# Partial sums and outputs of a matmul chain go through GpSimd's DMA queue

## The chip, the cores and the metric

One core of a Trainium2 chip runs the whole program. The metric is the device time of one execution in microseconds. Engines are named as the profile names them: PE (TensorE), DVE (VectorE), ACT (ScalarE), POOL (GpSimd) and SP (SyncE, which only issues DMAs).

## The reference

Attention through packed keys, then two feed-forward blocks, all in float32; 4608 tokens (8 batches of 576), model width 512.

```python
p_packed = softmax(p @ k.T / 8) @ v          # per head: 32 packed rows
a = softmax(q @ p_packed.T / 8) @ p_packed   # per head; 4608 x 512 in all
x = ((a @ w1) * (a @ w2)) @ w3 @ w_out       # 512 -> 1024 -> 1024 -> 512
h = x @ w_in                                 # 512 -> 2048
out = max(0.01 * h, h) @ w_out2              # 2048 -> 512
```

## The kernel before, in words

The program has two halves. The first (up to about 690 us) does the attention and the first feed-forward block and leaves `x2d`, the input of the second block, transposed, in DRAM. The change does not touch it. The last stage (lines 762 to 985) does the second block.

**Products.** A product of two float32 numbers is made of three fp32r matmuls (high x high, high x low, low x high; `PASSES`). Each matrix product is cut into 2 x 2 blocks and done with seven block products instead of eight (a Strassen-Winograd scheme), so operands come as seven "forms" m = 1 to 7, each a high and a low tile: `xh`, `xl` for the input, `wi` and `wo` for the weights, `gh`, `gl` for the activations. `ORDER` is the order of the seven products.

**Units.** The work is 18 units t = 0 to 17. The hidden width is cut into three parts F = 0, 1, 2 (`PARTS`; three, three and two chunks), and each part goes over the six token tiles of 768 columns (`NB = 6`). `h_unit(t)` makes the hidden activations of a unit (first matmuls, then leaky ReLU on ACT), `g_ops(t)` makes their seven forms on DVE and ACT, and `o_unit(t)` multiplies by `wo` and adds into four tiles `o` of 128 x 768 (384 KB each). Since the sum over hidden width is cut in three, the `o` of part 0 is stored to `part[0]` in DRAM, that of part 1 is fetched from `part[0]`, added to and stored to `part[1]`, and that of part 2 is fetched from `part[1]`, added to and stored to `out`. `begin_o(t)` allocates the four tiles and issues the fetches (line 936), the end of `o_unit(t)` issues the four stores (line 955). The pool holds `OB = 4` tiles `o`, one unit's worth: a fetch for the next unit needs a tile whose store has landed.

**Order.** The loop at line 959 does `begin_o(t-1)`, `h_unit(t)`, half of the loads of the next input forms, `o_unit(t-1)`, the other half, and `g_ops(t)`; the last unit of a part has its own `o_unit` directly behind that of the unit before. The Python order is a priority only: a list scheduler in the build sets the order on each engine from its own time estimates, so moving a DMA to another engine also changes the order of other instructions. On an engine, and on a queue, instructions are issued in that order; one that waits holds up what stands behind it.

**Queues.** In the last stage SP issues everything: the form loads (`load_forms`, line 797, `XF = 4` tiles each for `xh` and `xl`, seven forms a unit, so most loads wait for PE to be done with an older form), the weights (lines 787 and 825), the staging of later input tiles (lines 670 and 674, up to about 900 us), and the fetches and stores of `o`. POOL has nothing to do after 580.4 us. A matmul chain of `sevens` writes PSUM tiles `a`, `b` and `c` (2, 3 and 3 buffers); the additions into `o` and `gr` are DVE's (lines 842 and 847), some first copies are ACT's (line 844). DVE does in the last stage nothing but two-operand additions and subtractions.

Of the kernel before, what the change touches and what calls it, by code (L numbers as in the profile page):

```python
# [32 lines left out]
def tile_kernel(ctx, tc, qT, kT, vL, pT, w12, w3b, wo1, win, wo2, out):  # L33
    nc = tc.nc
# [599 lines left out]
    UT = 2 * HT  # L634
# [183 lines left out]
    part = dram.tile([2, DM, NT], F32, name="part")  # L818
# [60 lines left out]
    def run(dst, pairs, first, last):  # L879
        total = 3 * len(pairs)  # L880
        n = 0
        for lhs, rhs in pairs:
            for l, r in PASSES:
                nc.tensor.matmul(  # L884
                    dst, lhs(l), rhs(r), start=first and n == 0, stop=last and n == total - 1, skip_group_check=True
                )
                n += 1
# [39 lines left out]
    def begin_o(t):  # L927

        F, c0 = t // NB, t % NB * UT
        outs[t] = []  # L930
        for mb in range(2):
            for i in range(2):
                r = slice(i * 256 + mb * P, i * 256 + mb * P + P)
                o = b2.tile([P, 2, HT], F32, tag="o", name="o", bufs=OB)
                if F:
                    nc.sync.dma_start(out=o, in_=part[F - 1, r, c0:c0 + UT].rearrange("p (j c) -> p j c", j=2))
                outs[t].append((o, (out if F == 2 else part[F])[r, c0:c0 + UT].rearrange("p (j c) -> p j c", j=2)))

    def o_unit(t):
        F, n = t // NB, PARTS[t // NB][1]  # L940
        G = ops.pop(t)
        todo = outs.pop(t)
        chains = []
        for mb in range(2):
            def product(m, dst, first, last, mb=mb):
                run(
                    dst,
                    [(lambda l, c=c: wo[m][:, l, c, mb * P:mb * P + P], lambda l, c=c: G[m][l][:, c]) for c in range(n)],
                    first, last,
                )  # L950

            chains.append((product, lambda i, j, mb=mb: todo[2 * mb + i][0][:, j], F > 0))
        sevens(chains, None)
        for x in (1, 3, 0, 2):
            nc.sync.dma_start(out=todo[x][1], in_=todo[x][0])

    load_forms(0, ORDER[4:])
    STAGED = {0: ((3, 0),), 1: ((3, 1), (4, 0)), 2: ((4, 1), (5, 0)), 3: ((5, 1),)}
    for t in range(TB):
        F = t // NB  # L960
        start, end = t % NB == 0, t % NB == NB - 1
        if not start:
            begin_o(t - 1)
        if t == 0:
            load_wo(F)
        h_unit(t)
        if start:
            if t:
                load_wo(F)
            make_wo(F)  # L970
        if t + 1 < TB:
            load_forms(t + 1, ORDER[:4])
        if not start:
            o_unit(t - 1)
        if t + 1 < TB:
            load_forms(t + 1, ORDER[4:])
        g_ops(t)
        for f in (stage_b(*ua) for ua in STAGED.get(t, ())):
            for step in f:
                step()  # L980
        if end:
            begin_o(t)
            o_unit(t)
            if t + 1 < TB:
                make_wi(F + 1)
# [43 lines left out]
```

## Time and profile before

| | |
|---|---|
| device time, 3 runs | 1377.09, 1381.65, 1386.25 us; median 1381.65 |
| the profiled execution | 1377.09 us, of which 1375.3 us from the first instruction to the last |
| PE matmul busy | 1314.8 us (96%) |
| DVE, ACT, POOL busy | 956.6 us (70%), 703.3 us (51%), 185.8 us (14%) |
| DMA, all queues | 323.48 MB, mean 235 GB/s |
| SP's queue (q1) | 300.74 MB; its packets took 65.6% of the 16 DMA engines' span |

How to read it: the profiled execution took 1377.09 us, 4.56 us less than the median of the three runs. The granted clock of PE was 0.99 of 2.4 GHz over the span. A share of busy time is a mean over stages with different limits; the sections below go to the last stage alone. In a timeline row, the number in square brackets at the end is the time for which the engine stood idle before the first instruction of the row, and what ended that. SP's rows have no such number: the time between two of its rows is waiting. A row of busy time by stretch has: the stretch and its length in us; busy us (and number of instructions) of PE, PEld (weight loads), DVE, ACT and POOL; PE's granted clock; the DMA engines' busy share; GB/s. A row of waits has: who, for whom, us in total, times, the longest.

### The profile page before, as it was taken

To read this page: it belongs to the slowest core of one execution; us is meant where nothing else is said; L and a number is where in the kernel's file an instruction comes from. 1 tells how busy PE (TensorE), PEld (TensorE's weight loads), DVE (VectorE), ACT (ScalarE), POOL (GpSimd) and SP (SyncE) were. 2 spreads that over 40 slices of the span, in tenths; PEclk is the share of its full clock that TensorE was granted. 3 is DMA by queue.
4 is the path that set the end of the run, shared out by engine and by line. 5 is a ranking of instruction groups with operands and counts; after the bars stand their busy time and mean duration, and the time that the engine had idled before them with its cause. 6 is when DMAs were issued, how large, how long until landed. Compare 5 with 4: busy or idle time off the path is not lost.

```text
span 1375.3 us, 23473 instructions
## 1 busy us (share of the span) xinstructions
PE 1314.8 (96%) x8512; PEld 1256.7 (91%) x8512; DVE 956.6 (70%) x1588; ACT 703.3 (51%) x1365; POOL 185.8 (14%) x148
## 2 busy tenths in 40 slices
PE   6789999989999999999999999999999999999998
PEld 3578889988898999999999999998999999999997
DVE  4989777586778767863786676658665468496667
ACT  3576444565567545753755555536433335254432
POOL 1544540352025302300000000000000000000000
PEclk9899999999999999999999999999999999999999
DMA  9798785487777774187878975558447655778884
GB/s 291 261 314 290 238 278 181 119 273 253 250 229 248 243 236 153 47 273 251 278 256 297 322 280 206 203 177 283 152 160 240 207 175 181 256 276 306 290 288 149
DMA packets 174835, 323.48 MB, mean 235 GB/s; under 512 B 22656, under 2 KB 93312, under 8 KB 174720
## 3 DMA queue, kind: packets, MB, share of 16 engines
q1 hardware_dynamic: 153984, 300.74, 65.6%
q10 hardware_dynamic: 20736, 21.24, 4.5%
q8 instruction: 67, 1.10, 0.3%
q14 instruction: 48, 0.39, 0.1%
HBM read 226.75 MB, written 95.16 MB: 234 GB/s over the span
## 4 chain that ended last, share of the span: by engine, by line
PE 74%; DMA 10%; DVE 7%; issue 2%; ACT 1%; SPq 0%; POOL 0%; ACTq 0%; DVEq 0%; POOLq 0%
PE mm L105 26%; PE b L884 24%; PE c L884 13%; PE a L884 6%; DMA xh<-xfd 3%; PE m L105 2%; PE at L163 2%; DVE cT L282 1%; DMA xl<-xfd 1%; DVE M L108 1%; DVE cT L279 1%; DMA c<-wo 1%; PE at L215 1%; DMA c<-w3b 1%; DMA wi<-wid 1%
## 5 line engine op out<-in xcount | busy, mean ns | idle before, releaser
L105 PE MATMUL mm<-AT,M 128*128 128x288 f32 x1536 | 234.0, 304 | 22.5 <-DVE ab L451 11.1
L105 PEld LDWEIGHTS mm<-AT,M 128*128 128x128 f32 x1536 | 213.4, 192 | 36.3 <-DVE ab L451 14.3
L884 PE MATMUL b<-xh,wi 128*128 128x384 f32 x768 | 218.1, 336 | 6.2 <-DMA xh<-xfd 4.1
L884 PE MATMUL b<-gh,wo 128*128 128x384 f32 x768 | 213.6, 335 | 1.4 <-DVE o L847 1.4
L105 PEld LDWEIGHTS mm<-ab,W 128*128 128x128 f32 x1536 | 205.1, 189 | 7.7 <-issue 5.2
L105 PE MATMUL mm<-ab,W 128*128 128x288 f32 x1536 | 210.7, 297 | 1.3 <-DVE ab L108 1.3
L884 PEld LDWEIGHTS b<-xh,wi 128*128 128x128 f32 x768 | 140.5, 188 | 8.7 <-DMA xh<-xfd 4.5
L884 PEld LDWEIGHTS b<-gh,wo 128*128 128x128 f32 x768 | 140.3, 188 | 2.0 <-issue 1.0
L884 PE MATMUL b<-xl,wi 128*128 128x384 f32 x384 | 128.6, 335 | 0.0
L884 PE MATMUL b<-gl,wo 128*128 128x384 f32 x384 | 128.4, 334 | 0.0
L108 POOL TENSOR_TENSOR wsp<-c,wsp 128x512 fp32r<-128x512 f32 x54 | 73.2, 1358 | 279.1 <-ACT wsp L380 253.3
L656 ACT CAST gh<-gr 128x1152 fp32r<-128x1152 f32 (+1 forms) x72 | 75.6, 1052 | 68.9 <-PE b L884 32.2
L884 PE MATMUL c<-xh,wi 128*128 128x384 f32 x384 | 106.4, 336 | 3.3 <-DMA xh<-xfd 3.1
L884 PE MATMUL c<-gh,wo 128*128 128x384 f32 x384 | 107.3, 335 | 0.1
L108 DVE TENSOR_TENSOR gl<-gr,gh 128x1152 fp32r<-128x1152 f32 (+1 forms) x72 | 87.5, 1221 | 22.6 <-ACT gh L656 22.6
L108 DVE TENSOR_TENSOR M<-m,M 64x512 fp32r<-64x512 f32 x124 | 84.7, 686 | 22.8 <-ACT M L414 20.0
L656 ACT CAST gh<-gs 128x1152 fp32r<-128x1152 f32 (+1 forms) x54 | 56.9, 1054 | 61.7 <-PE b L884 32.3
L285 POOL TENSOR_TENSOR c<-cT,c 128x512 int32<-128x512 int32 x56 | 76.7, 1376 | 62.7 <-DVE cT L282 25.3
L832 ACT ACTIVATE gr<-gr 128x1152 f32<-128x1152 f32 (+1 forms) x54 | 57.3, 1062 | 47.9 <-DVE gr L847 47.6
L414 ACT CAST M<-m 64x512 fp32r<-64x512 f32 x124 | 71.5, 580 | 18.6 <-DVE M L108 5.4
L108 DVE TENSOR_TENSOR ab<-ab,ab 128x288 fp32r<-128x288 f32 x128 | 66.7, 550 | 15.2 <-ACT ab L430 14.9
L844 ACT COPY gr<-b 128x384 f32<-128x384 f32 x96 | 45.7, 479 | 58.2 <-PE b L884 56.8
(142 smaller groups left out, 2389.4 us busy)
## 6 DMA issues: line engine op xcount, KB each, us to landing
xh<-xfd SPq DMA_DIRECT2D x126, 384.0 KB, 5.3
xl<-xfd SPq DMA_DIRECT2D x126, 384.0 KB, 5.0
part<-o SPq DMA_DIRECT2D x48, 384.0 KB, 2.8
o<-part SPq DMA_DIRECT2D x48, 384.0 KB, 4.2
c<-wo SPq DMA_DIRECT2D x24, 512.0 KB, 5.7
c<-w12d SPq DMA_DIRECT2D x48, 256.0 KB, 3.5
abd<-ab ACTq DMA_DIRECT2D x80, 144.0 KB, 4.5
ab<-abd SPq DMA_DIRECT2D x80, 144.0 KB, 3.5
```

The costliest lines, as they stand in the source:

```text
L105: nc.tensor.matmul(dst, lhs(i), rhs(j), start=first and n == 0, stop=last and n == 2)
L108: engine.tensor_tensor(out=out, in0=x, in1=rd(hi), op=ALU.subtract)
L163: nc.tensor.matmul(ps[r:r + 64, th, :TH], w[:, 2 * g + j, :], x[:, th * TH:th * TH + TH], start=True, stop=True)
L215: nc.tensor.matmul(ps[r, :P], PT[:K, c, r], v[j][:K, c, :], start=c == 0, stop=c == 4)
L279: nc.vector.tensor_scalar(out=t, in0=hw, scalar1=3, scalar2=0x3FFFFFFF, op0=ALU.logical_shift_left, op1=ALU.bitwise_and)
L282: nc.vector.scalar_tensor_tensor(out=t, in0=hw, scalar=0xC0000000, in1=t, op0=ALU.bitwise_and, op1=ALU.bitwise_or)
L285: return lambda: nc.gpsimd.tensor_tensor(out=q, in0=t.bitcast(I32), in1=q, op=ALU.add)
L414: nc.scalar.copy(m[r, 0], ps[h ^ n][r])
L656: nc.scalar.copy(hi[step], x[step])
L832: nc.scalar.activation(out=out, in_=x, func=AF.Prelu, alpha=0.01)
L844: nc.scalar.copy(out, ps)
L884: nc.tensor.matmul(dst, lhs(l), rhs(r), start=first and n == 0, stop=last and n == total - 1, skip_group_check=True)
```

## The change

Two words change: the fetches of old partial sums and the stores of `o` are issued by POOL (`nc.gpsimd`) and no longer by SP (`nc.sync`). Sizes, buffers and semaphores' meaning stay.

```diff
--- before.py
+++ after.py
@@ begin_o
                 o = b2.tile([P, 2, HT], F32, tag="o", name="o", bufs=OB)
                 if F:
-                    nc.sync.dma_start(out=o, in_=part[F - 1, r, c0:c0 + UT].rearrange("p (j c) -> p j c", j=2))
+                    nc.gpsimd.dma_start(out=o, in_=part[F - 1, r, c0:c0 + UT].rearrange("p (j c) -> p j c", j=2))
@@ o_unit
         sevens(chains, None)
         for x in (1, 3, 0, 2):
-            nc.sync.dma_start(out=todo[x][1], in_=todo[x][0])
+            nc.gpsimd.dma_start(out=todo[x][1], in_=todo[x][0])
```

There are 48 fetches and 72 stores (48 of `part`, 24 of `out`). Numbers in the names below are those of the buffers; four `o` numbers in a row are the four tiles of one unit.

SP in the middle of part 1, while the tiles `o_12212` to `o_12218` of unit 8 are stored and those of unit 9 (`o_12596` to `o_12602`) are fetched; before:

```order
L936 DMA o_12596<-part_8477 128x768
L936 DMA o_12598<-part_8477 128x768
L797 DMA xl_12550<-xfd_78 128x768
L955 DMA part_8477<-o_12214 128x768
L797 DMA xh_12549<-xfd_78 128x768
L936 DMA o_12600<-part_8477 128x768
L955 DMA part_8477<-o_12218 128x768
L797 DMA xl_12554<-xfd_78 128x768
L797 DMA xh_12553<-xfd_78 128x768
L936 DMA o_12602<-part_8477 128x768
L797 DMA xh_12557<-xfd_78 128x768
L797 DMA xl_12558<-xfd_78 128x768
```

The same form loads on SP in the change:

```order
L797 DMA xl_12550<-xfd_78 128x768
L797 DMA xh_12549<-xfd_78 128x768
L797 DMA xl_12554<-xfd_78 128x768
L797 DMA xh_12553<-xfd_78 128x768
L797 DMA xl_12558<-xfd_78 128x768
L797 DMA xh_12557<-xfd_78 128x768
L797 DMA xl_12768<-xfd_78 128x768
L797 DMA xh_12767<-xfd_78 128x768
L797 DMA xl_12772<-xfd_78 128x768
L797 DMA xh_12771<-xfd_78 128x768
```

The stores and fetches have left, and the form loads stand one behind the other in nearly the old order (the last low and high form are swapped).

The end of the program: before, on SP, the stores of the last unit but one (`o_14956` to `o_14962`), the fetches and stores of the last (`o_15218` to `o_15224`):

```order
L955 DMA out<-o_14956 128x768
L936 DMA o_15218<-part_8477 128x768
L955 DMA out<-o_14960 128x768
L936 DMA o_15220<-part_8477 128x768
L955 DMA out<-o_14958 128x768
L955 DMA out<-o_14962 128x768
L936 DMA o_15222<-part_8477 128x768
L936 DMA o_15224<-part_8477 128x768
L955 DMA out<-o_15218 128x768
L955 DMA out<-o_15220 128x768
L955 DMA out<-o_15222 128x768
L955 DMA out<-o_15224 128x768
```

In the change, on POOL:

```order
L955 DMA out<-o_14956 128x768
L955 DMA out<-o_14960 128x768
L955 DMA out<-o_14958 128x768
L936 DMA o_15218<-part_8477 128x768
L936 DMA o_15220<-part_8477 128x768
L936 DMA o_15222<-part_8477 128x768
L955 DMA out<-o_14962 128x768
L936 DMA o_15224<-part_8477 128x768
L955 DMA out<-o_15218 128x768
L955 DMA out<-o_15220 128x768
L955 DMA out<-o_15222 128x768
L955 DMA out<-o_15224 128x768
```

The first two fetches of the last unit stood each behind one store; now three stores stand ahead of the first three fetches. The last fetch still stands behind all four stores.

PE at the end of the program, where `c_15280` is the product that ends with the addition into the last fetched tile, `o_15224`; before:

```order
L884 MATMUL b_15234<-gh_15197,wo6_8472 128x384
L884 MATMUL c_15280<-gh_15210,wo3_8476 128x384
L884 MATMUL c_15280<-gl_15211,wo3_8476 128x384
L884 MATMUL c_15280<-gh_15210,wo3_8476 128x384 x2
L884 MATMUL c_15280<-gl_15211,wo3_8476 128x384
L884 MATMUL c_15280<-gh_15210,wo3_8476 128x384
L884 MATMUL b_15234<-gh_15206,wo7_8474 128x384
L884 MATMUL b_15234<-gl_15207,wo7_8474 128x384
L884 MATMUL b_15234<-gh_15206,wo7_8474 128x384 x2
L884 MATMUL b_15234<-gl_15207,wo7_8474 128x384
L884 MATMUL b_15234<-gh_15206,wo7_8474 128x384
L884 MATMUL b_15234<-gh_15214,wo4_8475 128x384
```

In the change:

```order
L884 MATMUL b_15226<-gh_15214,wo4_8475 128x384
L884 MATMUL b_15226<-gl_15215,wo4_8475 128x384
L884 MATMUL b_15226<-gh_15214,wo4_8475 128x384 x2
L884 MATMUL b_15226<-gl_15215,wo4_8475 128x384
L884 MATMUL b_15226<-gh_15214,wo4_8475 128x384
L884 MATMUL c_15280<-gh_15210,wo3_8476 128x384
L884 MATMUL c_15280<-gl_15211,wo3_8476 128x384
L884 MATMUL c_15280<-gh_15210,wo3_8476 128x384 x2
L884 MATMUL c_15280<-gl_15211,wo3_8476 128x384
L884 MATMUL c_15280<-gh_15210,wo3_8476 128x384
L884 MATMUL b_15234<-gh_15214,wo4_8475 128x384
```

The last part of the product `c_15280` (with `wo3`) stood twelve matmuls ahead of the end; now it stands six ahead of it.

## Rows read from the trace of the kernel before

**Rows 1.** Busy time by stretch: parts 0, 1, 2 of the last stage, and the end.

```profile
690.00:968.00 278.00, 273.62 (x1565) 271.12 (x1565) 186.36 (x270) 152.22 (x256) 0.00 (x0) 1.00 0.72 250
968.00:1196.00 228.00, 226.00 (x1292) 223.88 (x1290) 142.55 (x201) 88.05 (x123) 0.00 (x0) 1.00 0.57 191
1196.00:1359.00 163.00, 159.18 (x905) 157.23 (x906) 117.23 (x191) 70.38 (x111) 0.00 (x0) 1.00 0.78 273
1359.00:1376.00 17.00, 10.73 (x56) 9.28 (x55) 8.50 (x15) 0.84 (x1) 0.00 (x0) 0.93 0.54 199
```

**Rows 2.** Waits of PE, 690 to 1376 us.

```profile
PE b L884 <- DMA xh<-xfd: 4.1, 4, 1.5
PE c L884 <- DMA xh<-xfd: 3.1, 3, 1.4
...
PE b L884 <- DVE o L847: 1.4, 2, 0.7
PE b L884 <- DVE o L842: 0.6, 1, 0.6
...
PE c L884 <- DMA xl<-xfd: 0.4, 2, 0.2
```

**Rows 3.** Waits of SP, the same stretch.

```profile
SPq L955 <- DVE o L847: 137.0, 29, 17.8
SPq L797 <- PE b L884: 86.2, 50, 6.7
SPq L936 <- DMA part<-o: 38.1, 19, 5.4
SPq L936 <- DMA out<-o: 35.4, 15, 6.9
```

**Rows 4.** SP's timeline, 1077 to 1091 us: start, length, instruction.

```profile
1077.99 0.38 SPq L955 DMA_DIRECT2D part<-o  x1
...
1083.63 0.32 SPq L936 DMA_DIRECT2D o<-part  x1
...
1088.37 0.32 SPq L936 DMA_DIRECT2D o<-part  x1
1088.78 0.38 SPq L797 DMA_DIRECT2D xh<-xfd  x1
```

**Rows 5.** PE's timeline: four matmuls that waited for a form.

```profile
936.76 0.44 PE L884 MATMUL c<-xh,wi 128*128 128x384 f32 x1 [1.41 <-DMA xh<-xfd]
...
1093.74 0.80 PE L884 MATMUL c<-xh,wi 128*128 128x384 f32 x3 [0.73 <-DMA xh<-xfd]
...
1197.37 0.45 PE L884 MATMUL b<-xh,wi 128*128 128x384 f32 x1 [1.51 <-DMA xh<-xfd]
...
1339.26 0.44 PE L884 MATMUL c<-xh,wi 128*128 128x384 f32 x1 [1.00 <-DMA xh<-xfd]
```

**Rows 6.** Busy time by stretch, the turn from part 1 to 2.

```profile
1190.00:1206.00 16.00, 13.66 (x74) 12.32 (x72) 6.59 (x13) 7.70 (x15) 0.00 (x0) 1.00 1.00 368
```

**Rows 7.** Lines 936 (fetch) and 955 (store): ns min/median/max of an issue; us to landing.

```profile
L936 SPq DMA_DIRECT2D o<-part x48: 319/320/555, 916.9 to 1362.5; - x48
...
DMA to landing us min/median/max: 3.2/4.2/7.7
...
DMA to landing us min/median/max: 2.3/3.1/7.7
```

**Rows 8.** Lines 285 (POOL) and 279 (DVE): ns min/median/max.

```profile
L285 POOL TENSOR_TENSOR c<-cT,c x56: 1260/1292/1932, 31.2 to 537.8; 128x512 int32<-128x512 int32 x56
...
L279 DVE TENSOR_SCALAR cT<-c x72: 387/427/1518, 9.0 to 460.4; 128x512 uint32<-128x512 uint32 x72
```

**Rows 9.** Waits of DVE, 690 to 1376 us: those for a fetch.

```profile
DVE o L842 <- DMA o<-part: 10.7, 7, 2.2
```

**Rows 10.** The end: timeline of SP (last stores) and of DVE (last addition).

```profile
1364.40 8.05 SPq L955 DMA_DIRECT2D out<-o  x4
...
1371.53 0.56 DVE L842 TENSOR_TENSOR o<-b,o 128x384 f32<-128x384 f32 x1 [1.42 <-PE b L884]
```

## The prediction, made before the changed kernel was run

> **What bounds the kernel now.** I read the busy time by stretch first, since the change acts in the last stage alone. In its three parts PE works 273.62 of 278 us, 226.00 of 228 and 159.18 of 163 [rows 1]; the reader is to see that 10.2 us are all that PE leaves idle there, at the full clock. Only the last 17 us have more (6.3 us), most of it behind the last matmul. So this stage is PE's own work, and no rearrangement of DMAs can give back more than those 10.2 us and a little of the end.
>
> The waits of PE come next. Form loads (`xh`, `xl`) cost it 4.1 + 3.1 + 0.4 = 7.6 us in nine waits; additions into `o` that came late cost 1.4 + 0.6 = 2.0 us [rows 2]. These two are what the change can touch.
>
> Then SP's waits: 137.0 us for an addition that must end before a store, 38.1 + 35.4 us for a store that must land before a fetch reuses its tile, and 86.2 us for PE to give a form tile back [rows 3]. The last would stay; the first three, 210 us, hold form loads behind them only where a form tile is free meanwhile. SP's timeline shows one such place: a store goes out at 1077.99, the fetch that needs its landing stands until 1083.63, the next such fetch until 1088.37, and only then, at 1088.78, goes the load of a high form [rows 4]. PE waits for it until 1093.74, for 0.73 us [rows 5].
>
> **What moves and what it costs.**
>
> *The form loads.* 120 DMAs leave SP. Their issue, 0.32 us each [rows 7], was 38 us of SP's time and is worth nothing by itself: SP has hundreds of us of waiting. What counts is the standing. Of PE's waits for forms, three (1.41 us at 936.76, 0.73 at 1093.74, 1.00 at 1339.26 [rows 5]) follow the pattern of [rows 4], a fetch that waits for a landing a few loads ahead on SP, of which there are these three; I take all of their 3.1 us back. The other 4.5 us I take back by half, 2.2 us: there SP did not stand for a landing just before, and the load was slow to land, with stores and fetches ahead of it in the same queue. The clearest, 1.51 us at 1197.37 [rows 5], lies in a stretch where the DMA engines are busy all of the time, at 368 GB/s [rows 6]: the bytes stay, so not all of it can go. Gain: 5.3 us, with bounds of 0 and 7.6.
>
> *What a transfer costs on POOL.* No row shows a DMA that POOL issues. I call p the time by which one lands later than from SP. Below: landings reach 7.7 us against a least of 3.2 for a fetch and 2.3 for a store [rows 7], because form loads stand ahead in the queue; on a queue of its own a transfer could land sooner, and with medians of 4.2 and 3.1 that is p = -0.8 to -1.0 us. Above: POOL's nearest work, one instruction on 128 partitions, takes 1.29 us, up to 1.93 where DVE is at the same time at work [rows 8]; if making the transfer takes that in place of 0.32 us, p is 1.0 to 1.6 us, and 2.9 if it also stands behind one just like it. I take p = 1.0 us, by the row's median, since mostly one transfer is made at a time. The Trainium skill ("DMA: Bandwidth & Descriptors", section Latency and other measured facts) gives about 1 us to the first byte from GpSimd against 0.6 from SP; with that p would be 0.4 us and the sum 2.5 us lower; no row here shows it.
>
> *The turn of a tile `o`.* Store, landing, fetch, landing, first addition: each turn has two transfers, so 2p = 2.0 us more. In parts 0 and 1 most turns have time: what a fetch brings is used much later, and only seven additions in the whole stage waited for one, for 10.7 us in all [rows 9], at five units (t = 11, 13, 14, 16 and 17), while PE lost 2.0 us by `o` [rows 2]: a fifth. PE has three buffers each of `b` and `c` to run ahead into. Four of these units (the last is counted below) at 2.0 us make 8.0 us more waiting of DVE, and by that fifth 1.6 us of PE. Bounds: 0, if the landings get as much quicker as p costs, and 8.0, if PE's slack is used up.
>
> *The end.* Last addition at 1371.53, last store behind it [rows 10]: that store lands p later, 1.0 us, with nothing to hide it. Ahead of it, the last fetched tile has a turn of 2p = 2.0 us more, while the order gives its product six matmuls more time, at 159.18 / 905 = 0.18 us each [rows 1] 1.1 us: 0.9 us remain. That the first fetch of the last unit now stands behind the store of `o_14958` costs, I think, nothing: the additions into it stand later on DVE too; its cover is the order, and if that is wrong it is one landing of 3.2 to 4.2 us [rows 7]. Sum of the end: 1.9 us.
>
> *Sum.* -5.3 + 1.6 + 1.9 = -1.8 us, on the profiled execution's 1377.09 us 1375.3. That execution was 4.56 us under the median of its three runs; I apply the change to the median, 1381.65 - 1.8 = 1379.9, and say **1380 us**.
>
> **The rivals.**
>
> *A. As above, no change that can be measured:* 1380 us. With the gain at 7.6 us, the turns at nothing and the last store 0.8 us sooner it is 1373; with no gain, the turns at 8.0 us and the end at 1.9 it is 1392. Chance 0.56. About 1%, 13.8 us, is what a measurement of this kernel tells from no change.
>
> *B. The forms come no sooner.* SP's loads wait 86.2 us for PE's tiles [rows 3], which no queue changes, and the bytes stay. Then the gain is 0 and the costs 3.5 us: 1385 us. Against it speak [rows 4], where the load stood behind two landings. Beside it stands a rule of the Trainium skill ("DMA: Bandwidth & Descriptors", section Issuing engines are not separate DMA queues): all queues run on the same 16 engines, and issuing from more of them saves only the issuing time. By that rule B is the whole story; the trace agrees for 1190 to 1206 us and speaks against it at 1077 to 1089, where a queue stood still for a semaphore. Chance 0.20.
>
> *C. Slower: the turn of `o` becomes the bound.* The place is part 2 and the turn from part 1 to 2, where additions already wait for fetches [rows 9]. POOL makes its transfers while DVE works, and where both worked at once in this trace each held up the other: POOL's instruction takes 1.29 us in the middle and up to 1.93, DVE's 0.43 and up to 1.52 [rows 8]. On top of that POOL's queue holds a fetch behind stores that are not ready. With p = 2.9 us and PE losing all that DVE loses, five turns of 2p make 29 us and the last store 2.9; less the 5.3 of the forms that is +26.6 us: 1408 us. It decides against no change from 11p = 13.8 + 5.3, p = 1.7 us. For it: the seven waits, and that PE's slack of some us at each is unknown. Against: PE lost only a fifth of what DVE lost, and the landings get a queue of their own. The Trainium skill ("SBUF — State Buffer", section Who interferes with whom) says that GpSimd is shut out only by DVE's two-port modes or, where it reads, by two SBUF inputs, and infers that descriptors escape a `tensor_tensor`, which is all that DVE does in this stage; by that rule p stays near 1 us and C does not happen; no run here shows it yet. Chance 0.16.
>
> *D. Faster, all waits gone:* both lines of waits, 7.6 + 2.0 us [rows 2], go and the end costs nothing: 1372 us. Against: that asks for p below 0 in a stage with 0.78 of the DMA engines busy [rows 1]. Chance 0.07; a time more than 13.8 us lower would ask for more than PE's idle 10.2 us and is as good as excluded.
>
> *E. It does not do what it says:* the order shows the stores and fetches on POOL and no longer on SP, so only an order elsewhere that happens to be worse or better could be the cause. Chance 0.01.
>
> **How the numbers follow.** Predicted is A's time, 1380 us. The range 1370 to 1396 holds A with its bounds, B, D and the lower part of C, and leaves out C's upper part and noise at the low side, less than 2 in 10. Slower by over 1% (above 1395.5) is C but for its lower part, 0.13, and a bit of B: 0.14. Faster by over 1% (below 1367.8) is only a chance of the order: 0.03. Within 1%: 0.83.
>
> **What would show it.** In the changed profile, PE's waits for `xh` and `xl` fall from 7.6 to some 2 to 3 us, and SP waits almost only for PE; if they stay at 7, B is right. The fetch line, now on POOL, shows landings: a median under 5.2 us (4.2 + p) agrees with p up to 1 us; 6 us and more is C, and DVE's waits for fetches then go from 10.7 us to over 30. PE's busy time in the last stage stays where it is within 1 us, and DVE's additions keep their 0.56 us. The last store lands about 1 us later behind the last addition. What would make the prediction wrong is a PE that waits for `o` in every unit of part 2, or a first fetch of the last unit that comes so late that the end stands for it.

## The result, and the profile after

The changed kernel took 1386.94 us (median of 9 runs, 1382.83 to 1390.94), the kernel before 1379.24 us beside it: a ratio of 1.0068, 95% interval 1.0048 to 1.0088. By the ratio it is 9 us slower (the medians are 7.7 us apart), within 1%, where 1.8 us less were forecast. A second measurement (e15 below) gave 1.0045, 1.0027 to 1.0063. The profiled execution took 1387.15 us and spans 1385.4 us, 10.1 more than before. Of these, 0.9 us lie ahead of the stage that the change touches: its first matmul starts at 653.1 us, before at 652.2. In e15, the same program, it starts at 647.9, so moments and lengths of two executions are to be held against each other with care.

Busy time by stretch, with the columns of [rows 1]; the last stretch ends with the program:

```profile
690.00:968.00 278.00, 272.77 (x1558) 269.98 (x1557) 186.02 (x269) 152.09 (x255) 15.35 (x28) 1.00 0.72 249
968.00:1196.00 228.00, 224.02 (x1278) 221.37 (x1278) 143.15 (x202) 84.56 (x117) 24.12 (x44) 1.00 0.55 187
1196.00:1359.00 163.00, 159.25 (x905) 156.86 (x905) 113.69 (x186) 71.16 (x113) 20.26 (x37) 1.00 0.78 275
1359.00:1386.00 27.00, 17.43 (x88) 16.17 (x86) 13.86 (x24) 3.35 (x4) 6.01 (x11) 0.86 0.53 173
```

PE lost 0.9 us more in part 0 and 2.0 us more in part 1; the end is 10 us longer. Part of that length is work which the delays ahead pushed into it: 88 matmuls fall into it, not 56. Its mean granted clock is 0.86 instead of 0.93; over half of what is missing lies behind the last matmul, where it costs nothing (0.65 from 1380 to 1386 us).

PE's waits, to be held against [rows 2]:

```profile
PE b L884 <- DMA xh<-xfd: 6.7, 6, 2.9
PE b L884 <- DVE o L842: 3.2, 2, 2.3
PE c L884 <- DMA xh<-xfd: 2.3, 3, 1.4
...
PE b L884 <- DMA xl<-xfd: 0.7, 1, 0.7
```

With two small rows that are left out (0.2 us for a form, 0.5 us for `o`) the forms cost 9.9 us (7.6 before) and late additions into `o` 3.7 us (2.0 before). SP's waits, beside [rows 3]:

```profile
SPq L797 <- PE b L884: 126.4, 54, 5.4
SPq L797 <- PE a L884: 117.8, 17, 23.3
SPq L797 <- PE c L884: 58.1, 31, 6.1
```

SP is freed as the change meant: the 210 us of waits for additions and landings are gone. What grew is its waiting for PE to give tiles back; the row for `b` stood at 86.2 us. And the line that fetches and the line that stores, now on POOL, beside [rows 7]:

```profile
L936 POOL DMA_DIRECT2D o<-part x48: 548/553/557, 920.6 to 1372.5; - x48
...
DMA to landing us min/median/max: 3.5/5.8/7.9
...
L955 POOL DMA_DIRECT2D part<-o x48: 542/544/689, 715.0 to 1201.2; - x48
...
DMA to landing us min/median/max: 2.6/3.6/9.0
```

A transfer holds POOL for 0.55 us (SP: 0.32), and in the best case lands 0.3 us later than from SP (3.5 against 3.2, 2.6 against 2.3). A store also starts 0.3 us after its addition: the last addition ends at 1379.85 + 0.56 = 1380.41, the store starts at 1380.71; before, both stood at 1372.1.

```profile
1379.85 0.56 DVE L842 TENSOR_TENSOR o<-b,o 128x384 f32<-128x384 f32 x1 [0.49 <-PE b L884]
```

Undisturbed, p is therefore 0.6 us. The medians rose by more, 4.2 to 5.8 and 3.1 to 3.6 us.

### The profile page after: what moved, and what is told of

Its sections match the earlier page's. It is cut to its first block, busy times and chain, and to the rows that moved or that the text cites. A ratio compares the mean times of both kernels' runs of the same rounds, so it can differ in the third digit from the quotient of the medians.

```text
span 1385.4 us, 23473 instructions
## 1 busy us (share of the span) xinstructions
PE 1319.2 (95%) x8512; PEld 1260.5 (91%) x8512; DVE 959.1 (69%) x1588; ACT 702.8 (51%) x1365; POOL 249.9 (18%) x268
## 4 chain that ended last, share of the span: by engine, by line
PE 65%; DMA 12%; DVE 8%; issue 5%; ACT 2%; POOL 1%; SPq 1%; ACTq 0%; POOLq 0%; DVEq 0%
PE mm L105 22%; PE b L884 22%; PE c L884 11%; PE a L884 6%; DMA xh<-xfd 5%; DMA c<-win 2%; PE m L105 2%; PE at L163 1%; PE at L215 1%; DVE M L108 1%; DMA xl<-xfd 1%; DVE cT L282 1%; DVE cT L279 1%; DMA c<-w3b 1%; DVE gl L108 1%
## 5 line engine op out<-in xcount | busy, mean ns | idle before, releaser
L955 POOL DMA_DIRECT2D part<-o x48 | 26.3, 547 | 517.7 <-DVE o L847 484.8
```

The costliest lines, as they stand in the source:

```text
L955: nc.gpsimd.dma_start(out=todo[x][1], in_=todo[x][0])
```

## The experiments

All ratios are to the kernel before, from runs on the same chip. "The turn" in the table is that from unit 6 to 7, the first at which both stores and fetches run; its numbers are the landing of the high form that PE wants next there, and PE's idle time in front of it, both from the trace. An interval is about 2.5 us to either side, and the waits of two executions of one program differ by some us, so a profile alone does not decide a total; a wait that comes back at the same place in every kernel of a kind is taken as its doing.

| run | on POOL | ratio (95%) | landing, us | PE idle, us |
|---|---|---|---|---|
| before | nothing | 1 | 6.3 | 0 |
| the change | all | 1.0068 (1.0048 to 1.0088) | 9.8 | 2.9 |
| e15 | all, again | 1.0045 (1.0027 to 1.0063) | 8.8 | 1.8 |
| e1 | all but the last unit's fetches | 1.0037 (1.0022 to 1.0052) | 10.3 | 3.4 |
| e5 | all but the end | 1.0017 (0.9997 to 1.0038) | 9.2 | 2.2 |
| e4 | units of parts 0 and 1 | 1.0028 (1.0012 to 1.0045) | 9.1 | 2.2 |
| e16 | that turn alone | 1.0027 (1.0010 to 1.0045) | 9.3 | 0.9 |
| e12 | all but end and part 1's fetches | 1.0002 (0.9982 to 1.0021) | 6.4 | 0 |
| e7 | stores of parts 0 and 1 | 0.9988 (0.9970 to 1.0006) | 6.2 | 0 |
| e2 | all stores | 1.0028 (1.0008 to 1.0048) | 5.8 | 0 |
| e3 | all fetches | 1.0059 (1.0036 to 1.0081) | 8.3 | 0 |
| e13 | the end alone | 1.0026 (1.0007 to 1.0045) | 6.3 | 0 |
| e14 | the end alone, on ACT | 1.0000 (0.9982 to 1.0019) | 6.3 | 0 |
| e8 | all, on ACT | 1.0009 (0.9989 to 1.0029) | 7.0 | 0 |

In e2, e7 and e12 the order on SP puts this high form ahead of its low form; the low form then lands 7.3, 7.8 and 7.7 us after its own issue. From the first issue of the pair to the later landing it is 6.7 us before, 7.7 to 8.1 us in these three and 10.3 us in the change, so their rows look better than they are.

Four names run through the expectations: **order** (three stores now stand ahead of the last unit's first fetches), **making** (a transfer that POOL makes comes late), **sharing** (a second queue shares the DMA engines with the form loads) and **packets** (POOL's packets are the larger ones, so its queue gets the larger share).

### The end

**e1, last fetches back on SP.**

```diff
-                    nc.gpsimd.dma_start(out=o, in_=part[...
+                    (nc.sync if t == 17 else nc.gpsimd).dma_start(out=o, in_=part[...
```

> Only the four fetches of the last unit (t = 17) go back to SP; all stores and the other fetches stay on POOL. The changed kernel was 1.0068 times the kernel before (about +9 us). In its trace PE waits 3.7 us for additions into o in the last 20 us, then runs nine matmuls at 0.32 us in place of 0.17, and 5.6 us follow its last matmul in place of 3.8. Theory 'order' (three stores stand ahead of the first three fetches of the last unit on POOL): with nothing ahead of them the fetches land in time, PE's waits for o at the end fall below 1.5 us, the slow matmuls go, the time is 3 to 4 us under the change (ratio to before near 1.004); the last store is still 0.5 us or more late. Theory 'making' (POOL's transfers are late by themselves): the fetches now come from SP but wait for landings of stores made by POOL, so half of it comes back, 1 to 2 us (1.0055). Theory 'sharing' (a second queue takes DMA time from the form loads): nothing at the end hangs on it, 1.0068 stays.

Measured: 1.0037, as order expected. PE's waits for `o` fell to 1.4 us, but the run moved the end in another way too: POOL issues the last three stores together (1377.24 to 1378.85), and the program ends 6.3 us behind the last addition (before: 3.2). **e5, the last stores too**, in the order of the changed kernel:

```diff
+                    (nc.sync if t == 17 else nc.gpsimd).dma_start(out=o, ...
+            (nc.sync if t >= 16 else nc.gpsimd).dma_start(out=todo[x][1], ...
```

> The stores of units 16 and 17 and the fetches of unit 17 are on SP; all else is on POOL as in the change. On SP the build puts the same three stores ahead of the first three fetches as on POOL in the change. 'Order': PE still waits 2 to 4 us for o in the last 20 us, and only the tail behind the last matmul shortens, by about 1 us: ratio near 1.006. 'Making': transfers by SP land 0.3 us and more sooner each and the issue takes 0.3 us less, so PE's waits for o at the end go back to 1.5 us and the tail to 4 us: ratio near 1.003. 'Sharing': the rest of the stage is unchanged, so PE's waits for xh and xl stay at 9 to 11 us whatever the end does.

Measured: 1.0017, below what order expected and near making; PE's waits for forms were 5.8 us, not the 9 to 11 that sharing expected. SP issued the last transfers in the same order as POOL had, three stores ahead of three fetches, and most of the cost was gone: order falls as its cause. The first eight of the same twelve transfers, first on POOL in the changed kernel (timeline: start, length, instruction, idle time before it and what ended that):

```profile
1357.78 0.55 POOL L955 DMA_DIRECT2D out<-o  x1 [11.03 <-DVE o L847]
1359.98 1.08 POOL L955 DMA_DIRECT2D out<-o  x2 [1.65 <-DVE o L847]
1361.29 0.55 POOL L936 DMA_DIRECT2D o<-part  x1 [0.23 <-DMA out<-o]
1363.74 0.55 POOL L936 DMA_DIRECT2D o<-part  x1 [1.89 <-DMA out<-o]
1367.24 0.56 POOL L936 DMA_DIRECT2D o<-part  x1 [2.95 <-issue]
...
1372.45 0.55 POOL L936 DMA_DIRECT2D o<-part  x1 [4.11 <-DMA out<-o]
```

and then on SP in e5:

```profile
1355.80 3.42 SPq L955 DMA_DIRECT2D out<-o  x3
1359.71 2.65 SPq L936 DMA_DIRECT2D o<-part  x3
1363.71 0.34 SPq L955 DMA_DIRECT2D out<-o  x1
1366.88 0.32 SPq L936 DMA_DIRECT2D o<-part  x1
```

From the first store to the last fetch SP takes 11.1 us, POOL 14.7 us. One piece of that is the third fetch: its store had landed at 1364.4 by the trace, yet POOL stood until 1367.24, for 2.95 us that ended with nothing that the profile shows. What hangs on it, on PE in the changed kernel:

```profile
1371.83 0.69 PE L884 MATMUL b<-gh,wo 128*128 128x384 f32 x1 [2.27 <-DVE o L842]
1372.32 0.52 PE L884 MATMUL b<-gl,wo 128*128 128x384 f32 x1
```

After the 2.27 us of idleness the matmuls come 0.32 us apart instead of 0.17 until 1374.9, and the granted clock is 0.66 in the mean:

```profile
1371.00:1376.00 5.00, 4.17 (x15) 4.17 (x16) 2.83 (x6) 0.00 (x0) 1.09 (x2) 0.66 0.53 172
```

With two levels, 2.4 and 1.2 GHz, that mean makes 3.4 us at the lower one; eight steps took 2.6 us in place of 1.4, 1.2 us on top of the wait. e15 has the same behind its wait, 3.4 us at the lower level from 1363.5.

**e13, the end alone on POOL**, and **e14, the end alone on ACT's queue**; up to some 30 rows at the end PE's order is that of the kernel before:

```diff
-                    nc.sync.dma_start(out=o, ...
+                    (nc.gpsimd if t == 17 else nc.sync).dma_start(out=o, ...
-            nc.sync.dma_start(out=todo[x][1], ...
+            (nc.gpsimd if t >= 16 else nc.sync).dma_start(out=todo[x][1], ...
```

> The kernel before, with the end alone moved to POOL: the stores of the last two units and the fetches of the last. The order on PE and DVE is that of the kernel before but for some 30 rows at the very end. If the end is worth most of the change's cost (the ratio 1.0068 fell to 1.0017 when the end went by SP), the ratio is 1.003 to 1.006, 4 to 8 us over before; the last stage up to its last 30 us is as before. If the end only costs where the rest goes by POOL too, the ratio is under 1.002.

> The same end moved to ACT's queue in place of POOL's. If the cost of the end is POOL's own lateness (0.55 us for a transfer on POOL, 0.3 us before a store starts, 0.3 us more to landing, and whatever holds POOL beside these), it is gone: ratio 0.998 to 1.001. If it is the order, or a queue apart from SP's, it stays: 1.003 and above.

Measured: 1.0026 (3.6 us) and 1.0000. So the end costs by itself, and not because it is a queue apart: on ACT's no cost is measured. PE's idle times at the end, e13:

```profile
1366.35 0.41 PE L884 MATMUL c<-gh,wo 128*128 128x384 f32 x1 [1.93 <-DVE o L842]
...
1373.37 0.44 PE L884 MATMUL c<-gh,wo 128*128 128x384 f32 x1 [1.04 <-DVE o L842]
```

and e14, the same matmuls:

```profile
1360.58 0.41 PE L884 MATMUL c<-gh,wo 128*128 128x384 f32 x1 [0.19 <-DVE o L842]
...
1366.73 0.44 PE L884 MATMUL c<-gh,wo 128*128 128x384 f32 x1 [0.73 <-DVE o L842]
```

The two waits for a fetched tile grow by 1.74 + 0.31 = 2.05 us on POOL. The last four fetches land in 4.1 us at the median there, in 3.3 from ACT. Behind the last addition (ends 1378.30 and 1371.68) the program takes another 4.2 us on POOL and 3.2 us on ACT, to spans of 1382.5 and 1374.9. Waits and tail make 3.05 us of the 3.6. Of the 1.0 us of the tail, the store starts 0.3 us and lands another 0.3 us later; the rest comes behind the last landing. There stands the program's closing (line 1025), with an instruction named DRAIN on every engine. POOL's began with its last store and took 3.2 us in e13, the longest of its three; in e14 the last of them took under 0.1 us (its longest, 1.4 us, is that at 578 us):

```profile
L1025 POOLq DRAIN  x3: 40/102/3175, 1378.6 to 1382.3; - x3
...
L1025 POOLq DRAIN  x3: 40/82/1421, 578.0 to 1374.6; - x3
```

In the changed kernel it takes 3.5 us, and the program ends 1.8 us behind the last landing (0.8 before).

**e15, the changed kernel once more.**

> The changed kernel once more, beside the same runs of the kernel before as the other three, and for a second profile. The ratio should be 1.005 to 1.009. PE's wait of 2 to 3 us for a form at the turn from unit 6 to 7 should be there again. POOL's 2.95 us before the third fetch of the last unit, which ended with nothing that the profile shows, comes again if it is a property of the program, and is absent if it was chance of that execution; then the wait of 2.3 us of PE for `o` at the end is shorter too.

Measured: 1.0045, a little under what was expected, its interval well into that of the first. POOL's stop was there again:

```profile
1358.61 0.56 POOL L936 DMA_DIRECT2D o<-part  x1 [2.96 <-issue]
```

It belongs to the program, then, and not to one execution; PE waited 2.5 us for `o` behind it. Its cause stays open: e13, with another order, does not have it.

### The middle

**e16, the turn from unit 6 to 7 alone**: eight transfers on POOL.

```diff
+                    (nc.gpsimd if t == 7 else nc.sync).dma_start(out=o, ...
+            (nc.gpsimd if t == 6 else nc.sync).dma_start(out=todo[x][1], ...
```

> The kernel before, with one turn alone moved to POOL: the stores of unit 6 and the fetches of unit 7, eight transfers. 'Sharing' expects the form loads at that turn to land in 8 to 10 us against 6.3 us before, and PE to wait for a form there for 1 to 3 us, so a ratio of 1.000 to 1.003. If the wait there needs the other transfers on POOL as well, the loads land within 7 us and PE waits for nothing.

The two form loads in question in the kernel before (low and high form, issued at 991.0 and 991.5):

```profile
DMA to landing us min/median/max: 5.8/6.0/6.3
```

in the changed kernel (issued at 993.7 and 994.1), with who waited for them:

```profile
  PE b L884: 2.9, 1
...
DMA to landing us min/median/max: 7.8/8.8/9.8
```

and in e16:

```profile
  PE b L884: 0.9, 1
...
DMA to landing us min/median/max: 7.8/8.6/9.3
```

So eight transfers are enough to make the load 3.0 us later. What moved while the high form was in flight (packets, MB, share of the engines, a packet at the edge counted whole), before, from 991.46 to 997.76:

```profile
q1 hardware_dynamic: 865, 2.35, 100.9%
```

and in the changed kernel, from 994.14 to 1003.97, POOL's queue first:

```profile
q0 software_dynamic: 339, 1.60, 50.6%
q1 hardware_dynamic: 627, 1.74, 46.0%
```

The engines were as good as full in both, and half of them worked for POOL. In the changed kernel POOL issued these around the loads:

```profile
993.17 0.55 POOL L936 DMA_DIRECT2D o<-part  x1
993.71 0.54 POOL L955 DMA_DIRECT2D part<-o  x1
996.77 0.55 POOL L936 DMA_DIRECT2D o<-part  x1 [2.52 <-DMA part<-o]
```

The fetch at 996.77 went out 2.6 us after the high form and landed at 1003.8, before it (1004.0). On SP's one queue that fetch stood behind the forms and landed after them, at 998.8 against 997.8, though it is the one that has time: its addition came some 16 us after the landing. That is sharing, but not all of the 3.5 us. POOL's second fetch and last store went out 1.0 and 0.4 us ahead of the high form; on SP's one queue it was 2.0 and 1.2 us, so more of them had already moved. In all 1.0 MB more moved before the form landed, by my estimate 2.7 us at the 376 GB/s of before. The other 0.9 us is a hole: from 995.5 to 996.75 the engines moved 81 GB/s with five transfers in flight. e15 (115 GB/s from 988.7 to 989.9) and e16 (169 GB/s from 994.2 to 995.4) have it too, the kernel before does not while its load is in flight; its cause is open. PE idles longer in the changed kernel than in e16 because its order there wants the form eight matmuls earlier. The ratio of e16, 3.7 us, is more than the 0.9 us at the turn. Its trace shows where most of the rest may lie, at the turn from part 1 to 2:

```profile
1199.53 0.58 PE L884 MATMUL b<-xh,wi 128*128 128x384 f32 x2 [1.76 <-DMA xh<-xfd]
...
1206.17 0.44 PE L884 MATMUL c<-xh,wi 128*128 128x384 f32 x1 [2.65 <-DMA xh<-xfd]
```

These are 4.4 us (before 2.3, e13 2.1, e14 2.0), and from 1200 to 1212 the granted clock is 0.86 in the mean. Nothing is on POOL there in e16; what differs from the kernel before is the order that the build made. So the price of sharing at this turn is the 0.9 us here, and up to 3.4 us in the other kernels of the table; the ratio holds the altered order as well.

**e4, POOL in parts 0 and 1 only.**

```diff
+                    (nc.gpsimd if t < 12 else nc.sync).dma_start(out=o, ...
+            (nc.gpsimd if t < 12 else nc.sync).dma_start(out=todo[x][1], ...
```

> Stores and fetches go by POOL only in the units of parts 0 and 1 (t below 12); in part 2 and at the end they go by SP, as in the kernel before. If the cost is a second queue that shares the DMA engines with the form loads ('sharing'), parts 0 and 1 keep the changed kernel's waits of PE for forms (some 9 us there against 5.6 us before), part 2 and the end lose their cost, and the time is 3 to 4 us over the kernel before: 1379 to 1380 us against 1376 us. If the cost is only that a transfer made by POOL comes late ('making'), parts 0 and 1 have time for that (a fetch is used some 20 us later), and the time is that of the kernel before within 1 us.

Measured: 1.0028, 3.9 us: as sharing expected. PE waited 2.2 us at the turn. But it also waited 2.7 us at 1202 to 1210 and 2.3 us at 1286 for forms, in part 2, where e4 has nothing on POOL; how much of the 3.9 us is sharing and how much the altered order is not shown.

**e7, only the stores of parts 0 and 1**: `(nc.gpsimd if t < 12 else nc.sync)` at the stores alone.

> Only the stores of parts 0 and 1 (48 of 120 transfers) go by POOL; all fetches, and everything in part 2, go by SP. The run with all stores on POOL had the waits of part 1 for forms at 0.7 us instead of 3.4 us. If a store that waits for its addition on SP holds up form loads, as the prediction had it, this version keeps that gain without the cost at the end: 2 to 3 us below the kernel before, 1373 to 1375 us. If that low number was chance, or if sharing eats it, the time is that of before within 1 us, 1376 us.

Measured: 0.9988, no difference that can be told. PE does not wait at the turn, though the stores alone make the pair of forms 1.4 us later there (8.1 against 6.7 us). Waits for forms are 5.9 us in all: a gain, if there is one, is below what the interval can tell.

**e12, both places back on SP**: the fetches by `(nc.gpsimd if 12 <= t < 17 else nc.sync)`, the stores by `(nc.sync if t >= 16 else nc.gpsimd)`.

> The traces so far put the changed kernel's loss in two places: the turn from unit 6 to 7, where PE waits 2.9 us for a form that shares the DMA engines with fetches, and the end. Here both are undone: the fetches of part 1 and those of the last unit go by SP, the stores of the last two units too; the other stores and the fetches of part 2 stay with POOL. If the two places are the whole cost, the time is that of the kernel before within 2 us (1375 to 1379 us against about 1377 us), and PE's wait for a form at the turn from unit 6 to 7 is gone. If the loss is spread over all transfers that POOL makes, 80 of 120 still go by POOL and 4 us or more of the 8 to 9 us stay: 1381 us or above.

Measured: 1.0002. With 80 of 120 transfers still on POOL no cost is left that can be told; it sits at the end, 3.6 us (e13), and where stores and fetches both go by POOL in the middle, 3.9 us (e4); together these make 7.5 us, between the 6.2 and 9.4 of the two measurements of the change.

**e2 and e3, one half of the change each**: only the stores on POOL, and only the fetches.

> All 72 stores on POOL, all 48 fetches on SP as before. The fetches again stand on SP for a store's landing and hold form loads up. 'Sharing': stores and form loads are in flight together from two queues, so PE's waits for xh and xl stay above the 7.6 us of before, near 9; ratio 1.002 to 1.006. If instead the standing of SP were what costs (the thought behind the forecast), the waits would be like before's, 7 to 8 us. 'Order': no store stands ahead of a fetch on one queue, so PE's waits for o at the end stay near 2 us. 'Making': 72 of 120 transfers, all in the turn of o: ratio 1.003 to 1.005.

> All 48 fetches on POOL, all 72 stores on SP. SP now stands for additions (137 us before) but not for landings. 'Sharing': only fetches share with form loads; part 0 has no fetch, so its PE waits for forms are like before's (about 1.7 us from 690 to 900 us), those of parts 1 and 2 are up; ratio 1.001 to 1.004. 'Order': no store ahead of a fetch on POOL, PE's waits for o at the end near 2 us, tail as before: near 1.000. 'Making': fetches 0.3 us later each at five tight turns: under 2 us, 1.001. If freeing SP of landings is worth what was forecast (5.3 us), the ratio is 0.997 to 0.999.

Measured: 1.0028 and 1.0059. e2 costs as much as e13, but in another place: its last store (1372.64) lands after 2.7 us, and the program ends 4.6 us after that, at 1379.9. POOL's closing DRAIN takes 6.5 us here:

```profile
L1025 POOLq DRAIN  x3: 40/93/6516, 1372.6 to 1379.6; - x3
```

With it the program takes 7.5 us behind the last addition (before 3.2), which covers the 3.9 us of the ratio; PE's waits for forms are down to 4.7 us. Why the DRAIN goes on for 3.8 us after the last landing is open. e3 lies above all that was expected of it and has other places: PE waits 4.0 us at 1336 and 3.1 us at 1365 for `o`, and from 1363 to 1376 us the granted clock is 0.61 in the mean.

### Whose queue, and how large a piece

**e8, stores and fetches on ACT's queue**: `nc.scalar` in place of `nc.gpsimd`.

> Stores and fetches go by ACT's queue in place of POOL's: a second queue as well, but one whose issues take no time of POOL. 'Sharing' expects PE's waits for forms as in the changed kernel, 10 us or more, and form loads that land late (9 in 10 within 7.6 us in part 1, against 6.2 us before). 'Making' expects the waits for forms and the landings of before (7.6 us and 6.2 us), and the time at most 2 us over the kernel before, 1378 us. A third thing can cover both: a store that waits for its addition on ACT holds ACT's copies of products behind it; then PE's waits for ACT grow from 1.5 us to 10 us and more and the time is above 1390 us. The landings of the form loads still tell the two theories apart.

Measured: 1.0009. The load at the turn lands in 7.0 us, between SP's one queue (6.3) and POOL's (9.8), so a second queue costs something here whoever fills it, and POOL's most. PE's waits for forms are 5.6 us, under both expectations. The third thing of the expectation is there, but smaller:

```profile
PE b L884 <- ACT gr L844: 6.1, 5, 2.7
```

**e10, the other way round**: `(nc.gpsimd if t >= 6 else nc.sync)` at the form loads, the rest on SP.

> The other way round: the form loads of parts 1 and 2 (t from 6) go by POOL, stores and fetches stay with SP. 'Packets' expects that the form loads now have the larger share where both queues have work: 9 in 10 land within 6.8 us in part 1 (6.2 us before, and some 0.6 us because POOL makes them), no wait at the turn from unit 6 to 7, fetches at a median over 5 us, the end as before, and a time of 1376 to 1380 us. 'Making' expects that each of the 170 loads comes 0.6 us late to a PE that has little to spare: waits for forms grow from 7.6 us to 12 us or more, and the time is 1382 us or above.

Measured: 1.0039 (1.0018 to 1.0060), as making expected, but not by its waits: forms cost 6.8 us, `o` 6.6 us. The forms did not land sooner (7.2 us for 9 in 10 in part 1); now SP's fetches are late beside them.

**e6, one queue again, on POOL**: `(nc.gpsimd if t else nc.sync)` at the forms and `(nc.gpsimd if F else nc.sync)` at the weights too.

> One queue again, but POOL's: the form loads of all units but the first and the weights of parts 1 and 2 go by POOL too, so that they stand in one queue with stores and fetches as before, each made by POOL. 'Sharing' expects that PE's waits for forms fall from the changed kernel's 9.9 us to the 7 or 8 us of before or less, since in one queue a load isn't cut up with transfers that were issued after it; with the late end kept (about 5 us) the time is 1381 to 1383 us. 'Making' expects that every load comes some 0.6 us later and that POOL's 0.55 us for each of 400 transfers adds up where several stand together: waits for forms stay at 10 us or grow, and the time is at 1386 us or above.

Measured: 1.0178 (1.0141 to 1.0215), as making expected. But the waits for forms fell to 5.4 us, as sharing expected, and the loss is another:

```profile
PE b L884 <- ACT gr L844: 7.8, 4, 4.5
```

The waits for ACT and DVE over 1.5 us lie before 950 us, in part 0, where inputs are still staged; why ACT and DVE are late there is open. Another 6 us lie at the end, where POOL's closing DRAIN takes 9.0 us. The run decides nothing on the whole time.

**e9 and e11, each transfer in two**, by columns and by rows; all on POOL.

```diff
+                    for j in range(2):
+                        nc.gpsimd.dma_start(out=o[:, j], in_=part[F - 1, r, c0 + j * HT:c0 + j * HT + HT])
```

> As the changed kernel, but each store and fetch is two transfers of 384 columns, so that a row is 1536 bytes and no longer 3072. In the changed kernel POOL's packets are of 6144 bytes and SP's of 3072, and where both queues have work they alternate packet by packet. If that gives POOL two thirds of the engines ('packets'), and if the packets shrink to 3072 with the rows, the form loads at the turn from unit 6 to 7 land in 7 to 8 us and no longer in 9.8 us, PE's wait there falls from 2.9 us to under 1.5 us, and waits for forms fall from 9.9 us to 8 us or less. If the number of transfers counts ('making': 0.55 us each on POOL, now 240), fetches land later, waits for `o` grow from 3.7 us to 6 us or more, and the time is 1388 us or above. If the packets stay at 6144 bytes the first part is not tested.

> As the changed kernel, but each store and fetch is two transfers of 64 rows: the number of transfers doubles as in the run with column halves, the rows stay at 3072 bytes. 'Packets' expects packets of 6144 bytes as in the changed kernel and its waits: form loads of over 9 us at the turn from unit 6 to 7 and waits for forms at 9 to 11 us. 'Making' expects the same as for the column halves, 1388 us or above.

Measured: 1.0000 (0.9984 to 1.0016) and 1.0286 (1.0263 to 1.0309). The queues' traffic in part 1 (packets, MB, share of the engines): in the changed kernel

```profile
q1 hardware_dynamic: 11504, 25.56, 33.2%
q0 software_dynamic: 3433, 16.90, 21.3%
```

and in e9

```profile
q1 hardware_dynamic: 12243, 26.66, 33.1%
q0 software_dynamic: 5857, 18.04, 24.1%
```

POOL's packets (q0) are larger than SP's (q1), 4.9 KB in the mean against 2.2, counting the small ones; with columns halved 3.1 KB. The loads at that turn then land in at most 6.1 us, and by the ratio no cost is left. The landing is what "packets" expected; the waits for forms, 9.1 us elsewhere, are not, and e9 also changes the order on every engine. It is not shown that the packets do it. Making as a matter of the number of transfers falls with e9: 240 transfers, no loss. In e11 the same 240 cost 39 us, 7 of them behind the last landing, with a closing DRAIN of 10.4 us, and its waits for forms are 23 us where packets expected 9 to 11.

## Why the prediction was wrong

**The form loads (−5.3 us forecast, bounds 0 and −7.6): the step that failed.** It counted what a load gains by no longer standing behind a store or a fetch, and not what it loses to them as neighbours. The gain is small: of the waits of [rows 5] that I took back, 1.41, 0.73 and 1.00 us (3.1 in all; 2.7 and 3.3 in e13 and e14, which have the same order there), the changed kernel keeps 1.18, 0.23 and 0.67, and e15 0.6 in all. But two new ones stand beside them, at 829 and 1004 us:

```profile
829.25 0.44 PE L884 MATMUL c<-xh,wi 128*128 128x384 f32 x1 [1.41 <-DMA xh<-xfd]
...
936.03 0.44 PE L884 MATMUL b<-xh,wi 128*128 128x384 f32 x1 [1.18 <-DMA xh<-xfd]
...
1004.01 0.44 PE L884 MATMUL b<-xh,wi 128*128 128x384 f32 x1 [2.86 <-DMA xh<-xfd]
```

The late load of the one at 1004 is shown to come from the eight transfers of that turn (e16). The one at 829 comes, with 1.4 to 1.7 us, in every run of the table that has the stores of part 0 on POOL (e1, e2, e4, e5, e7, e12, e15) and in none that has them on SP (0.5 us at most); the wait at 863 (1.2 us before) is gone in them. The stores' queue and the altered order change there together, so which of them does it is not shown. In two executions the change had 9.9 and 6.6 us of waits for forms; in three executions with the order of before (before, e13, e14) they were 7.6, 8.2 and 8.4. So the gain is nothing, give or take 2 us, and the bound of 0 left out a loss such as that at the turn. Rival B's "no sooner" was the better forecast, by a stronger mechanism than it gave. The Trainium skill ("DMA: Bandwidth & Descriptors", section Issuing engines are not separate DMA queues) says that all queues interleave on the same engines; the turn agrees, 6.3 us against 9.8. The Trainium skill ("DMA: Bandwidth & Descriptors", section Queues, rings and completion order) says that an engine goes round among its queues packet by packet; that fits a fetch which overtakes a form issued 2.6 us earlier, and the 63 packets of POOL's queue beside 59 of SP's from 998 to 999.25 us.

**p (1.0 us, bounds −1.0 to 2.9).** Undisturbed it is 0.6 us, and so the size was fair. The lower bound supposed that a queue of its own makes landings quicker; at the median they became slower, by 1.6 us for a fetch and 0.5 us for a store, as sharing would have it. By the prediction's own sign (a median under 5.2 us for p up to 1 us) the fetches' 5.8 us is too much: in company p is above 1 us for them. The Trainium skill ("DMA: Bandwidth & Descriptors", section Latency and other measured facts) has about 0.4 us between the two paths; the least landings here differ by 0.3.

**The turn of `o` (1.6 us).** DVE's waits for fetches [rows 9] became

```profile
DVE o L842 <- DMA o<-part: 11.1, 8, 2.6
```

and PE's for `o` 3.7 us, of which 0.94 + 0.17 + 2.27 us lie in the last unit: elsewhere the turns cost nothing, inside the bounds.

**The end (1.9 us): mis-sized.** By e13 it is 3.6 us (1.0 to 6.2). The tail grew by 1.0 us there, as said, but only 0.6 us of it is the last store; the rest is POOL's closing DRAIN, for which the sum had no term. The last fetched tiles cost 2 us of PE, not 0.9; that p comes in at each of several stores and fetches that follow on each other is my reading, and no run separates them. In the changed kernel the tail grew by 1.8 us (5.0 against 3.2), and POOL's 2.95 us and the slow matmuls (1.2 us) came on top, all unforeseen. That the first fetch behind the store of `o_14958` costs nothing was right as far as e5 shows: it has that order on SP, and PE's waits for `o` are 1.5 us.

**The rivals.** C did not happen: p was 0.6 us undisturbed and at the median, with 0.3 us for the start, 1.9 us for a fetch and 0.8 us for a store, 1.35 us in the mean of a turn and under C's 1.7; DVE's waits for fetches rose by 0.4 us only. The Trainium skill ("SBUF — State Buffer", section Who interferes with whom) infers that a two-operand addition does not hold up POOL's descriptors; the rows agree: 544 and 553 ns at the median and 689 at most, in parts in which DVE was busy for two thirds of the time. D fell with the gain. E, a worse order by itself, had a chance of 0.01 and is not excluded for a part of the middle: e16 and e4 wait longer than the kernel before where they have nothing on POOL. The time lies in the range, and within 1%, but not on the side forecast; that it lies there is owed to the width of the range, not to the sum.

## What to carry to other kernels

A queue that holds urgent loads behind lazy transfers also protects them: in one queue what was issued later landed later, while on a second queue a transfer that had 16 us to spare took its share of the engines from the load that PE wanted next. So before splitting queues, ask of each moved transfer what will be in flight beside it, and count on a loss as well as a gain. Where a chain of store, fetch and addition ends the program, keep it on the quickest issuer, and look behind the last landing too: the engine that issued the last stores may close late. A moved DMA also moves the order of everything else in such a build; compare a moved piece with the same piece on a third queue (e13 and e14) before naming the queue as the cause.

## What the runs showed that I had not expected

- The lateness of POOL's stores in the middle costs nothing that can be told (e7, e12: 0.9988 and 1.0002), nor does the end on ACT's queue (e14: 1.0000).
- POOL's closing DRAIN took 3.2 to 10.4 us in the runs whose last stores went by POOL; in e2 it went on for 3.8 us after the last landing, about the whole of that run's 3.9 us.
- Transfers of 64 rows were dear: in e11 the halves (192 KB) of a fetch landed in 6.3 us at the median in part 1, in e9, of equal bytes but 128 rows, in 4.8; stores 3.4 against 2.2.
- POOL can stop for 2.95 us ahead of a DMA with nothing in the profile to show for it, twice at the same instruction.
- A wait of 2.3 us on PE near the end was followed by 3.4 us at the lower clock level, which made it half as dear again.
